# First unit of a gated recurrence: its last head pair's gates and decays through the gaps and a DMA, and the second unit's first steps placed ahead of the first up-projection

## The chip, the cores and the metric

The kernel runs on one core of a Trainium2 chip. The core has TensorE (PE, with its weight loads PEld), VectorE (DVE), ScalarE (ACT), GpSimd (POOL) and SyncE (SP); SP and ACT issue the DMAs here. Times are device microseconds (us) of one execution. The kernel before takes 575.21 us, the median of three runs (574.94 to 575.88).

## The reference

A gated linear recurrence over 768 tokens, for 4 batches of 8 heads of size 48, then a two-layer network with an ELU on 3072 tokens of width 384. The network's two weights are float64, the rest is float32.

```python
f = 1.0 / (1.0 + np.exp(-f_logit))
for t in range(S):
    state = f[:, :, t, :, None] * state + np.einsum('bhd,bhe->bhde', k[:, :, t], v[:, :, t])
    y[:, :, t] = np.einsum('bhd,bhde->bhe', q[:, :, t], state)
x = y.transpose(0, 2, 1, 3).reshape(B * S, H * D)
h = x @ w_in                                    # 384 x 2048
g = np.where(h > 0.0, h, np.exp(np.minimum(h, 0.0)) - 1.0)
out = g @ w_out                                 # 2048 x 384
```

## The kernel before

**Units.** The tokens are cut into 12 units of 256. For each unit the recurrence becomes matmuls over four chunks of 64 tokens. Eight heads lie as four pairs (p = 0 to 3): a pair takes 96 of the 128 partitions, and 32 partitions are gaps. `gates` (L611) turns f's logits into 1/f with two ACT instructions, `grow` (L627) makes their running product with a scan on DVE, `fall` (L632) its reciprocal on DVE. `scale` (L621) multiplies a pair of k by the product and a pair of q by the reciprocal, on POOL. `transposed` (L672) transposes two pairs of k on PE and copies them to kn on ACT. `advance` (L728) makes the four state increments, `step` (L687) adds them up on DVE, `scores` (L704) and `mask` (L721) make the causal products within a chunk, `outputs` (L744) and `carried` (L762) the unit's output, which ACT copies to xt. For unit 0 `first_outputs` (L789) does the last two.

**Where pair 3 lives.** In unit 1 and later, the gates of pair 3 are not loaded as a pair of their own: they are loaded into the gap partitions of pairs 0 to 2, so that three scans and three reciprocals do all heads. `move` (L637) then copies them by two DMAs of 48 rows from the gaps to pair 3's place, once for the products (which = 0) and once for the reciprocals (which = 1). In the kernel before, unit 0 is the exception: all four pairs of f are loaded as they are, with four scans, four reciprocals and no move.

**Weights.** The float64 weights come in 16 items, sorted by when they are needed: item 0 is the first block of w_in, item 1 the second, item 2 the third, item 3 the first block of w_out. `fetch` (L537) loads one into one of seven places of `area`. `split` (L559, two DVE instructions), `lower` (L572, one on ACT) and `merge` (L578) make float32 words of it. merge runs on POOL for items from M0 = 3 on and on DVE for items 0 to 2, and then fetches the item seven further on. `bits`, which split writes and merge reads, has two buffers.

**Order.** The start is written out by hand (L1051 to L1131). `warm` (L1042) issues matmuls of 512 columns on the identity that compute nothing. From then on a loop of steps T runs over pairs of feed-forward blocks: an even T is an `up` (L928), an odd one from 5 on a `down` (L960) two blocks behind; `elu` (L943) is a DVE instruction after the two of ACT in `exped` (L921). What a plan holds for step T (`at_step`) is issued ahead of that step's up or down. A1 gives the steps of unit 1: transposes at its first number (before: at step 1, as a plan entry), then advance, steps, scores and mask, outputs, carried. Splits and lowers of the items from 2 on follow at the ends of steps, their merges in the plan. Engines run their instructions in this order, each waiting for semaphores. The DMAs of SP and ACT share eight semaphores, and a DMA that takes one over waits until the earlier DMA on it has landed.

**The start, in order.** ACT: unit 0's gates in three pieces, kn copies, unit 1's first half of the gates, the first state, lower(0), output copies, lower(1). DVE: memsets, four scans, four reciprocals, split(0), steps, mask, merge(0), the last step, unit 1's three scans, split(1), two reciprocals of unit 1, merge(1). SP: f, k, q of unit 0, f of unit 1, v, item 0, then k, q, v of unit 1, item 1, then item 7 (by merge(0)), the move of unit 1, items 2 to 6. PE: three warms, unit 0's transposes, one warm, advance of pairs 0 and 1, scores of pair 0, and so on with a warm between blocks, first_outputs, a warm, up(0).

Of the kernel before, what the change touches and what calls it, by code (L numbers as in the profile page):

```python
# [356 lines left out]
def fast(ctx: ExitStack, tc: tile.TileContext, q, k, v, f_logit, w_in, w_out, out, flag, outer):  # L357
# [18 lines left out]
    nc = tc.nc  # L376
# [18 lines left out]
    AHEAD = 7  # L395
    WA = 1
    M0 = 3
    Q1 = 4
    W0 = 3
    HOLD = 2  # L400
    A1 = (2, 4, 5, 7, 8, 9)
    D2 = (14, 16, 18, 20)
    A2 = (22, 24, 24, 26, 27, 28)
    D3 = (-7, -5, -3, -1)
# [25 lines left out]
    def load(u, names="fkqv"):  # L430
        b, s0 = u // UPB, (u % UPB) * U
        for n in names.replace("v", ""):
            to = qkf[u % NB][n][MAIN]
            frm = src[n][b, :, :, s0 : s0 + U].rearrange("(p r) d s -> (r d) p s", r=2)
            if n == "f" and u:
                to, frm = to[:, 0:NKT, 0], frm[:, 0:NKT]
            elif n == "f":
                to = to[:, :, 0]
            nc.sync.dma_start(out=to, in_=frm)
            for r in range(2 if n == "f" and u else 0):  # L440
                nc.sync.dma_start(
                    out=qkf[u % NB][n][GAP[r] : GAP[r] + PAD, 0:NKT, 0],
                    in_=src[n][b, 2 * NKT + r, :, s0 : s0 + U].rearrange("(i j) s -> i j s", i=PAD),
                )
        if "v" in names:
            nc.sync.dma_start(
                out=vs[u % NB][:, :, PAD : PAD + DM], in_=v[b, s0 : s0 + U].rearrange("(c t) n -> t c n", t=W)
            )
# [6 lines left out]
    def blank(i, *engines, zeros=None):  # L455
        for j, e in enumerate(engines):
            w = HP // len(engines)
            for n in "kq":
                e.memset(qkf[i][n][:, j * w : (j + 1) * w], 0.0)
        if i:  # L460
            (zeros or engines[-1]).memset(qkf[i]["f"][:, NKT], 1.0)
        else:
            engines[-1].memset(qkf[i]["f"][:, :, 0], 50.0)

    start = ctx.enter_context(ExitStack())
    start.enter_context(tc.manual_schedule())
# [92 lines left out]
    def split(n):  # L559

        if not wide or n >= NFT:
            return
        raw = raws[n]
        hi = raw.bitcast(I32)[:, 1::2]
        bits = held[n] = sb.tile([128, 2 * DM], I32, tag="bits", name=f"bits{n}")
        nc.vector.tensor_scalar(  # L566
            out=bits[:], in0=hi, scalar1=3, scalar2=0x3FFFFFF8,
            op0=ALU.logical_shift_left, op1=ALU.bitwise_and,
        )
        nc.vector.tensor_scalar(out=hi, in0=hi, scalar1=-(2**30), scalar2=None, op0=ALU.bitwise_and)  # L570

    def lower(n):  # L572

        if wide and n < NFT:
            raw = raws[n]
            nc.scalar.activation(raw.bitcast(U16)[:, 2::4], raw.bitcast(U32)[:, 0::2], AF.Copy, scale=2.0**-29)
# [34 lines left out]
    def gates(u, pieces=(NKT,), bias=1):  # L611

        p = 0
        for n in pieces:
            a = qkf[u % NB]["f"][:, p : p + n, 0]
            nc.scalar.activation(a, a, AF.Exp, scale=-1.0)
            if bias:
                nc.scalar.activation(a, a, AF.Copy, bias=1.0)
            p += n

    def scale(u, *todo):  # L621

        t = qkf[u % NB]
        for n, p, e in todo:
            e.tensor_tensor(out=t[n][:, p], in0=t[n][:, p], in1=t["f"][:, p, "kq".index(n)], op=ALU.mult)  # L625
# [6 lines left out]
    def fall(u, p):  # L632

        f = qkf[u % NB]["f"]
        nc.vector.reciprocal(f[:, p, 1], f[:, p, 0])  # L635
# [17 lines left out]
    def watch(u):  # L653
        nc.vector.scalar_tensor_tensor(
            out=fine[:], in0=qkf[u % NB]["f"][:, 0:NKT, 0, U - 1 :], scalar=LIMIT, in1=fine[:],
            op0=ALU.is_le, op1=ALU.mult,
        )

    def watch_last(u):
        nc.vector.scalar_tensor_tensor(  # L660
            out=fine[:, 0:1], in0=qkf[u % NB]["f"][:, NKT:, 0, U - 1 :], scalar=LIMIT, in1=fine[:, 0:1],
            op0=ALU.is_le, op1=ALU.mult,
        )

# [7 lines left out]
    def transposed(u, h, bank, pairs=(0, 1)):  # L672

        if 0 in pairs:
            pts[u, h] = ps.tile([128, 2, NW, 128], FP32, tag=bank, name=f"psT{u}_{h}")
            kns[u, h] = sb.tile([128, 2, NW, 128], FP32, tag="kn", name=f"kn{u}_{h}")
        for p in pairs:
            for w in range(NW):
                nc.tensor.transpose(  # L679
                    pts[u, h][:, p, w], in_=qkf[u % NB]["k"][:, 2 * h + p, w * W : (w + 1) * W], identity=ident[:]  # L680
                )
        p = slice(pairs[0], pairs[-1] + 1)
        nc.scalar.copy(kns[u, h][:, p], pts[u, h][:, p])
# [3 lines left out]
    def step(u, c):  # L687

        if u % UPB == UPB - 1 and c == NC - 1:
            return  # L690
        new = pus[u][c % 2][:, c // 2]
        box = boxes[(u * NC + c) % len(boxes)]
        s = box[:].rearrange("n (p d) -> n p d", d=64)[:, 0:HP, PAD:]
        if u % UPB or c:
            old = sts[u, c][:].rearrange("n (p d) -> n p d", d=64)[:, 0:HP, PAD:]
            nc.vector.tensor_tensor(out=s, in0=new, in1=old, op=ALU.add)
        else:
            nc.scalar.copy(s, new)
        if c == NC - 1:
            end = qkf[u % NB]["f"][:, :, 1, U - 1 :].broadcast_to([128, HP, D])  # L700
            nc.vector.tensor_tensor(out=s, in0=s, in1=end, op=ALU.mult)
        sts[(u, c + 1) if c < NC - 1 else (u + 1, 0)] = box

    def scores(u, banks=("a0", "a1"), pairs=range(HP), pc=None):  # L704

        t = qkf[u % NB]
        if pc is None:
            ats[u] = sb.tile([128, 2, NW, HP, C], FP32, tag="at", name=f"at{u}", bufs=1)
            pc = [ps.tile([128, NW, HP, C], FP32, tag=banks[r], name=f"psS{u}_{r}") for r in range(2)]
        for p in pairs:  # L710
            for w in range(NW):
                for b in range(2):
                    cols = slice(w * W + b * C, w * W + b * C + C)
                    for r in range(2):
                        nc.tensor.matmul(  # L715
                            pc[r][FULL[b], w, p], lhsT=t["k"][FULL[r], p, cols], rhs=t["q"][FULL[r], p, cols],
                            start=True, stop=True,
                        )
        return pc
# [322 lines left out]
    def warm(n, bank="m0"):  # L1042

        pw = ps.tile([128, 4, 128], FP32, tag=bank, name="psW")
        for _ in range(n):
            nc.tensor.matmul(  # L1046
                pw[:], lhsT=ident[:], rhs=ident[:].unsqueeze(1).broadcast_to([128, 4, 128]), start=True, stop=True
            )


    gates(0, (1, 1, 2))  # L1051
    fetch(0)
    load(1, "kqv")
    for n in range(1, HOLD):
        fetch(n)
    warm(W0, "m3")
    for p in range(HP):
        grow(0, p)
        scale(0, ("k", p, nc.gpsimd))
        transposed(0, p // 2, f"m{p // 2}", (p % 2,))  # L1060
    fall(0, 0)
    scale(0, ("q", 0, nc.gpsimd))
    warm(WA, "m3")
# [5 lines left out]
        vs[0][:, :, PAD : PAD + NKT * 2 * D].rearrange("t w (p r d) -> t w p r d", r=2, d=D)[:, :, :, 0],  # L1069
    )  # L1070
    fall(0, 1)
    scale(0, ("q", 1, nc.gpsimd))
    fall(0, 2)
    fall(0, 3)
    advance(0, (2,))
    warm(1)
    scores(0, None, (1,), pc)
    scale(0, ("q", 2, nc.gpsimd))
    advance(0, (3,))
    warm(1)  # L1080
    scores(0, None, (2,), pc)
    nc.gpsimd.tensor_copy(
        padded_v[:, :, :, PAD : 2 * PAD].rearrange("t w (r j) k -> t w r j k", r=2),
        vs[0][:, :, PAD + NKT * 2 * D : PAD + DM].rearrange("t w (r k j) -> t w r j k", r=2, j=NKT),
    )
    scale(0, ("q", NKT, nc.gpsimd))
    warm(1)
    scores(0, None, (NKT,), pc)
    warm(1)
    split(0)  # L1090
    for c in range(NC - 1):
        step(0, c)
    lower(0)
    mask(0, pc)
    merge(0)
    step(0, NC - 1)
    a = qkf[1]["f"][:, 0:NKT, 0]
    nc.vector.tensor_scalar_add(a, a, 1.0)
    for p in range(NKT):
        grow(1, p)  # L1100
    move(1, 0, nc.sync)
    split(1)
    for c in range(NC - 1):
        nc.gpsimd.tensor_copy(
            padded_s[:, c, :, PAD : 2 * PAD],
# [4 lines left out]
        nc.gpsimd.memset(area[:, HOLD:].bitcast(I32)[:, :, 0:1], 0)  # L1110
    for n in range(HOLD, AHEAD):
        fetch(n)
    first_outputs(0)
    first_outputs(1)
    warm(1)
    lower(1)
    fall(1, 0)
    scale(1, ("k", 0, nc.gpsimd), ("k", 1, nc.gpsimd), ("k", 2, nc.gpsimd), ("q", 0, nc.gpsimd))
    fall(1, 1)
    merge(1)  # L1120
    scale(1, ("k", NKT, nc.gpsimd))
    watch(0)
    watch_last(0)
    at_step(1, lambda: transposed(1, 0, "a0"), lambda: transposed(1, 1, "a1"))
    at_step(1, lambda: scale(1, ("q", 1, nc.gpsimd)))
    at_step(1, lambda: fall(1, 2))
    at_step(1, lambda: scale(1, ("q", 2, nc.gpsimd)))
    at_step(1, lambda: move(1, 1, nc.scalar))
    at_step(1, lambda: watch(1))
    at_step(Q1, lambda: scale(1, ("q", NKT, nc.gpsimd)))  # L1130
    attention(1, (), A1)  # L1131
    for n in range(1, NFT):
        t = max(needs[n][0] - 2, 0)
        if n > 1:
            at_step(t, lambda n=n: merge(n))
        if n > 1:
            later.setdefault(max(t - 2, 0), []).append(n)
    at_step(4, lambda: load(2))
# [89 lines left out]
```

## Time and profile before

| | |
|---|---|
| median of 3 runs | 575.21 us |
| the profiled execution | 574.94 us |
| its span in the trace | 573.2 us |
| PE busy | 552.4 us, 96% of the span |
| PEld / DVE / POOL / ACT busy | 502.8 / 394.0 / 292.0 / 229.9 us |
| mean granted clock of TensorE | 0.989 |
| PE's share of the chain of waits | 89% |
| first up-projection matmul (L937) starts | 29.34 us |
| first down-projection matmul (L969) starts | 46.64 us |

The busy time by stage gives for a stretch of the span how long each engine worked; where PE's number is the stretch itself, PE sets the pace. The chain of waits goes back from the last instruction through what released each. The timeline gives start, length, engine, line and operands, and in brackets how long the engine had been idle and who ended it.

### The profile page before, as it was taken

To read this page: it belongs to the slowest core of one execution; us is meant where nothing else is said; L and a number is where in the kernel's file an instruction comes from. 1 tells how busy PE (TensorE), PEld (TensorE's weight loads), DVE (VectorE), ACT (ScalarE), POOL (GpSimd) and SP (SyncE) were. 2 spreads that over 40 slices of the span, in tenths; PEclk is the share of its full clock that TensorE was granted. 3 is DMA by queue.
4 is the path that set the end of the run, shared out by engine and by line. 5 is a ranking of instruction groups with operands and counts; after the bars stand their busy time and mean duration, and the time that the engine had idled before them with its cause. 6 is when DMAs were issued, how large, how long until landed. Compare 5 with 4: busy or idle time off the path is not lost.

```text
span 573.2 us, 15184 instructions
## 1 busy us (share of the span) xinstructions
PE 552.4 (96%) x6220; PEld 502.8 (88%) x6220; DVE 394.0 (69%) x755; ACT 229.9 (40%) x419; POOL 292.0 (51%) x543
## 2 busy tenths in 40 slices
PE   5968899999999999999999999999999999999996
PEld 2546677777999999999999999999999999999996
DVE  6887555564794885786786776776786777655543
ACT  3265855443343343333433433343253243233331
POOL 7335536971357257257257347348348348325332
PEclk9899999999999999999999999999999999999999
DMA  7789970032006216216216206206206303201001
GB/s 193 192 234 281 217 228 16 2 92 74 24 10 152 84 37 153 85 35 153 85 23 166 86 12 176 86 9 179 85 3 172 99 2 77 77 9 35 29 1 35
DMA packets 37614, 53.07 MB, mean 93 GB/s; under 512 B 3584, under 2 KB 27360, under 8 KB 37536
## 3 DMA queue, kind: packets, MB, share of 16 engines
q1 hardware_dynamic: 36992, 51.62, 34.0%
q8 instruction: 51, 0.84, 0.6%
q10 hardware_dynamic: 544, 0.39, 0.3%
q14 instruction: 27, 0.22, 0.1%
HBM read 44.04 MB, written 4.72 MB: 85 GB/s over the span
## 4 chain that ended last, share of the span: by engine, by line
PE 89%; DMA 3%; DVE 3%; POOL 2%; issue 1%; ACT 1%; SPq 0%; ACTq 0%; DVEq 0%; POOLq 0%
PE psH L892 34%; PE psM L991 33%; PE psM L969 6%; PE psH L937 5%; PE psS L715 2%; PE psU_a L738 2%; PE psY L773 2%; PE psY L753 2%; PE psT L679 2%; DMA f<-f 1%; PE psW L1046 1%; DMA area<-in_moe_w_in_dram 1%; POOL wi L585 1%; DMA f<-in_f_logit_dram 1%; DVE bits L566 1%
## 5 line engine op out<-in xcount | busy, mean ns | idle before, releaser
L892 PE MATMUL psH<-xt,wi 128*128 128x128 f32 (+1 forms) x960 | 177.1, 293 | 0.0
L956 POOL TENSOR_TENSOR sums<-gg 128x128 f32<-128x128 f32 x160 | 69.6, 456 | 210.4 <-DVE gg L946 199.3
L892 PEld LDWEIGHTS psH<-xt,wi 128*128 128x128 f32 x960 | 135.9, 192 | 0.8
L924 ACT ACTIVATE gg<-hh 128x512 f32<-128x512 f32 x80 | 50.5, 631 | 205.4 <-DVE hh L914 137.9
L892 PE MATMUL psH<-xt,area 128*128 128x128 f32 x640 | 110.5, 275 | 0.0
L892 PEld LDWEIGHTS psH<-xt,area 128*128 128x128 f32 x640 | 96.9, 192 | 4.1
L901 DVE TENSOR_TENSOR hh<-psH,u 128x256 f32<-128x256 f32 x80 | 33.8, 422 | 88.8 <-ACT u L899 88.8
L991 PE MATMUL psM<-area,sums 128*128 128x192 f32 x480 | 91.1, 326 | 0.0
L991 PEld LDWEIGHTS psM<-area,sums 128*128 128x128 f32 x480 | 80.2, 190 | 0.0
L991 PE MATMUL psM<-wo,gg 128*128 128x192 f32 x320 | 68.1, 335 | 0.0
L635 DVE RECIPROCAL f<-f 128x256 f32<-128x256 f32 x37 | 64.2, 1745 | 1.0
L925 ACT ACTIVATE gg<-gg 128x512 f32<-128x512 f32 x96 | 60.6, 631 | 3.0
L946 DVE SCALAR_TENSOR_TENSOR gg<-gg,hh 128x512 f32<-128x512 f32 x80 | 55.7, 696 | 1.5 <-ACT gg L925 1.5
L991 PEld LDWEIGHTS psM<-wo,gg 128*128 128x128 f32 x320 | 50.2, 190 | 1.9
L914 DVE TENSOR_TENSOR hh<-psH,u43h 128x256 f32<-128x256 f32 (+1 forms) x160 | 49.6, 352 | 2.7
L937 PE MATMUL psH<-xt,wi 128*128 128x256 f32 x192 | 46.5, 394 | 1.9 <-DVE wi L585 1.1
L625 POOL TENSOR_TENSOR k<-k,f 128x256 f32<-128x256 f32 x48 | 40.0, 836 | 13.7 <-DVE f L630 13.0
L937 PEld LDWEIGHTS psH<-xt,wi 128*128 128x128 f32 x192 | 37.0, 196 | 10.4 <-ACT xt L830 1.3
L956 POOL TENSOR_TENSOR sums<-gg,sums 128x128 f32<-128x128 f32 x80 | 42.7, 534 | 6.3
L899 ACT COPY u<-psH 128x128 f32<-128x128 f32 x80 | 21.1, 264 | 59.4 <-PE psH L892 59.4
L969 PE MATMUL psM<-wo,gg 128*128 128x384 f32 x128 | 44.2, 488 | 0.0
L914 DVE TENSOR_TENSOR u43h<-psH,hh 128x256 f32<-128x256 f32 x80 | 33.8, 422 | 13.5 <-PE psH L892 13.1
(100 smaller groups left out, 746.5 us busy)
## 6 DMA issues: line engine op xcount, KB each, us to landing
area<-in_moe_w_out_dram SPq DMA_DIRECT2D x8, 768.0 KB, 6.5
again<-in_moe_w_in_dram SPq DMA_DIRECT2D x16, 384.0 KB, 4.3
again<-in_moe_w_out_dram SPq DMA_DIRECT2D x16, 384.0 KB, 3.5
k<-in_k_dram SPq DMA_DIRECT2D x12, 384.0 KB, 4.9
q<-in_q_dram SPq DMA_DIRECT2D x12, 384.0 KB, 5.9
v<-in_v_dram SPq DMA_DIRECT2D x12, 384.0 KB, 6.3
area<-in_moe_w_in_dram SPq DMA_DIRECT2D x8, 576.0 KB, 8.8
out_dram<-o SPq DMA_DIRECT2D x38, 96.0 KB, 1.7
```

Of the source, the lines that this page charges most:

```text
L625: e.tensor_tensor(out=t[n][:, p], in0=t[n][:, p], in1=t["f"][:, p, "kq".index(n)], op=ALU.mult)
L635: nc.vector.reciprocal(f[:, p, 1], f[:, p, 0])
L892: nc.tensor.matmul(to, lhsT=lhs, rhs=rhs, start=(n == 0), stop=True, skip_group_check=True)
L901: add = lambda to, x, y: nc.vector.tensor_tensor(out=to, in0=x, in1=y, op=ALU.add)
L914: add = lambda to, x, y: nc.vector.tensor_tensor(out=to, in0=x, in1=y, op=ALU.add)
L924: nc.scalar.activation(g[:], h, AF.Relu, scale=-1.0)
L925: nc.scalar.activation(g[:], g[:], AF.Exp, scale=-1.0)
L937: nc.tensor.matmul(ph[:, i], lhsT=wi[j][:, kt, i * 128 : (i + 1) * 128], rhs=xts[m][:, kt, :], start=(kt == 0), stop=(kt == NKT - 1),)
L946: nc.vector.scalar_tensor_tensor(out=g[:], in0=g[:], scalar=-1.0, in1=phs.pop(P), op0=ALU.add, op1=ALU.max)
L956: nc.gpsimd.tensor_tensor(out=s[:, i], in0=x, in1=y, op=op)
L969: nc.tensor.matmul(pm[t][:], lhsT=g[:, i, t * 128 : (t + 1) * 128], rhs=wo[:, 2 * j + i, :], start=(j == 0 and i == 0), stop=(j == NP - 1 ...
L991: nc.tensor.matmul(pm[bank][:, half * DH : (half + 1) * DH], lhsT=x, rhs=y, start=first, stop=(j == NP - 1), skip_group_check=True,)
```

## The change

All edits concern the first 60 us or so.

- Unit 0's f is loaded and blanked as that of the other units: pairs 0 to 2 and two small loads into the gaps, a memset of pair 3's place alone. Its gates are two pieces (pair 0, pairs 1 and 2) instead of three; it has three scans and three reciprocals, and two moves on ACT's queue (which = 0 after the first kn copies, which = 1 after the third reciprocal). `watch_last`, which looked at pair 3's last product, goes, as the gaps are watched with the others.
- k's pair 3 is scaled after the move, and its transpose stands after four warms. There are twelve warms in place of nine in the start.
- Unit 1's scans, its SP move and its first reciprocal come before unit 0's steps and mask; split(0), lower(0) and merge(0) come after the mask.
- The loop that fetches items 2 to 6 comes before merge(0), which fetches item 7.
- Unit 1's k scaling, transposes, third reciprocal and second move, which were partly plan entries of step 1, stand in the start ahead of up(0). Its q of pair 3 is scaled at step 1 instead of 4. merge(1) becomes a plan entry of step 0. A1 is (2, 3, 4, 6, 7, 9) instead of (2, 4, 5, 7, 8, 9).

M0, the item from which GpSimd merges, is 3 in both kernels.

```diff
-    A1 = (2, 4, 5, 7, 8, 9)
+    A1 = (2, 3, 4, 6, 7, 9)
...
-            if n == "f" and u:
+            if n == "f":
                 to, frm = to[:, 0:NKT, 0], frm[:, 0:NKT]
-            elif n == "f":
-                to = to[:, :, 0]
             nc.sync.dma_start(out=to, in_=frm)
-            for r in range(2 if n == "f" and u else 0):
+            for r in range(2 if n == "f" else 0):
...
-        if i:
-            (zeros or engines[-1]).memset(qkf[i]["f"][:, NKT], 1.0)
-        else:
-            engines[-1].memset(qkf[i]["f"][:, :, 0], 50.0)
+        (zeros or engines[-1]).memset(qkf[i]["f"][:, NKT], 1.0)
...
-    gates(0, (1, 1, 2))
+    gates(0, (1, 2))
...
-    for p in range(HP):
+    for p in range(NKT):
         grow(0, p)
         scale(0, ("k", p, nc.gpsimd))
-        transposed(0, p // 2, f"m{p // 2}", (p % 2,))
+        if p < 2:
+            transposed(0, 0, "m0", (p,))
+    move(0, 0, nc.scalar)
+    transposed(0, 1, "m1", (0,))
     fall(0, 0)
...
-    scale(0, ("q", 1, nc.gpsimd))
+    scale(0, ("k", NKT, nc.gpsimd), ("q", 1, nc.gpsimd))
     fall(0, 2)
-    fall(0, 3)
+    move(0, 1, nc.scalar)
+    warm(4)
+    transposed(0, 1, "m1", (1,))
     advance(0, (2,))
-    warm(1)
     scores(0, None, (1,), pc)
     scale(0, ("q", 2, nc.gpsimd))
     advance(0, (3,))
-    warm(1)
     scores(0, None, (2,), pc)
...
-    scale(0, ("q", NKT, nc.gpsimd))
-    warm(1)
-    scores(0, None, (NKT,), pc)
-    warm(1)
-    split(0)
-    for c in range(NC - 1):
-        step(0, c)
-    lower(0)
-    mask(0, pc)
-    merge(0)
-    step(0, NC - 1)
     a = qkf[1]["f"][:, 0:NKT, 0]
     nc.vector.tensor_scalar_add(a, a, 1.0)
     for p in range(NKT):
         grow(1, p)
     move(1, 0, nc.sync)
-    split(1)
+    scale(0, ("q", NKT, nc.gpsimd))
+    warm(2)
+    scores(0, None, (NKT,), pc)
+    warm(1)
+    fall(1, 0)
+    for c in range(NC - 1):
+        step(0, c)
+    mask(0, pc)
+    step(0, NC - 1)
+    split(0)
...
     for n in range(HOLD, AHEAD):
         fetch(n)
+    fall(1, 1)
     first_outputs(0)
+    lower(0)
+    merge(0)
     first_outputs(1)
+    scale(1, ("k", 0, nc.gpsimd), ("q", 0, nc.gpsimd), ("k", 1, nc.gpsimd), ("k", 2, nc.gpsimd))
+    scale(1, ("k", NKT, nc.gpsimd))
+    split(1)
+    transposed(1, 0, "a0")
     warm(1)
+    transposed(1, 1, "a1")
     lower(1)
-    fall(1, 0)
-    scale(1, ("k", 0, nc.gpsimd), ("k", 1, nc.gpsimd), ("k", 2, nc.gpsimd), ("q", 0, nc.gpsimd))
-    fall(1, 1)
-    merge(1)
-    scale(1, ("k", NKT, nc.gpsimd))
     watch(0)
-    watch_last(0)
-    at_step(1, lambda: transposed(1, 0, "a0"), lambda: transposed(1, 1, "a1"))
-    at_step(1, lambda: scale(1, ("q", 1, nc.gpsimd)))
-    at_step(1, lambda: fall(1, 2))
-    at_step(1, lambda: scale(1, ("q", 2, nc.gpsimd)))
-    at_step(1, lambda: move(1, 1, nc.scalar))
-    at_step(1, lambda: watch(1))
-    at_step(Q1, lambda: scale(1, ("q", NKT, nc.gpsimd)))
+    scale(1, ("q", 1, nc.gpsimd))
+    fall(1, 2)
+    scale(1, ("q", 2, nc.gpsimd))
+    move(1, 1, nc.scalar)
+    watch(1)
+    at_step(1, lambda: scale(1, ("q", NKT, nc.gpsimd)))
     attention(1, (), A1)
     for n in range(1, NFT):
         t = max(needs[n][0] - 2, 0)
-        if n > 1:
-            at_step(t, lambda n=n: merge(n))
+        at_step(t, lambda n=n: merge(n))
```

More of the change, by code (lines that the diff above doesn't have):

```diff
@@ L397, in fast @@
     M0 = 3
-    Q1 = 4
     W0 = 3
     HOLD = 2
-    A1 = (2, 4, 5, 7, 8, 9)
+    A1 = (2, 3, 4, 6, 7, 9)
     D2 = (14, 16, 18, 20)
@@ L655, in watch @@
             out=fine[:], in0=qkf[u % NB]["f"][:, 0:NKT, 0, U - 1 :], scalar=LIMIT, in1=fine[:],
[L656 to L661, printed above, removed]
             op0=ALU.is_le, op1=ALU.mult,
```

## The prediction

> **What bounds the kernel now.** I read the busy time by stage first. The columns are the stretch, its length, then busy us and instruction count of PE, PEld, DVE, ACT and POOL, then the granted clock.
>
> ```profile
> core 0: us, PE busy (x) PEld busy (x) DVE busy (x) ACT busy (x) POOL busy (x), PEclk, DMA share, GB/s
> 8.40:11.80 3.40, 1.20 (x5) 0.40 (x4) 2.91 (x4) 1.78 (x4) 2.77 (x3) 0.97 1.12 278
> 11.80:18.20 6.40, 5.73 (x71) 3.40 (x72) 6.40 (x5) 1.49 (x3) 3.97 (x8) 0.50 1.10 242
> 29.34:42.30 12.96, 8.27 (x97) 6.56 (x97) 11.50 (x15) 7.42 (x7) 4.30 (x5) 1.00 0.93 236
> 42.30:45.60 3.30, 3.30 (x8) 2.67 (x9) 3.11 (x3) 1.91 (x4) 1.92 (x1) 0.50 1.07 291
> 45.60:65.30 19.70, 16.41 (x237) 11.70 (x236) 14.20 (x21) 14.26 (x14) 11.33 (x7) 1.00 1.00 271
> 65.30:75.00 9.70, 9.70 (x41) 7.06 (x38) 3.46 (x5) 7.85 (x10) 3.64 (x3) 1.00 0.67 131
> ```
>
> From 65.3 us on PE does not idle again before the tail of the last output. Before that it has holes, and its clock is halved twice, after a stretch with few matmuls each time. So the change is worth the time by which it moves the start of the full stretch. I read the chain of waits next (start, length, what), for the early holes.
>
> ```profile
> 1.79 0.90 POOL f L463
> 2.69 0.02 issue
> 2.71 3.87 DMA f<-in_f_logit_dram
> ...
> 31.12 5.20 DMA area<-in_moe_w_in_dram
> ...
> 40.05 6.88 DMA f<-f
> ...
> 47.74 1.86 POOL wi L585
> 49.61 0.02 issue
> 49.63 2.19 DVE bits L566
> ```
>
> Three transfers carry it: the first gates, which wait for a memset; the third weight item; and unit 1's moved decays. The timeline shows why the third item is late, and whom it stops.
>
> ```profile
> 24.79 0.39 SPq L547 DMA_DIRECT2D area<-in_moe_w_out_dram  x1
> ...
> 28.48 1.30 SPq L642 DMA_DIRECT2D f<-f  x2
> ...
> 29.87 0.53 SPq L549 DMA_DIRECT2D area<-in_moe_w_in_dram  x1
> ...
> 39.34 1.16 ACT L683 COPY kn<-psT 128x512 f32<-128x512 f32 x2
> ...
> 40.07 0.31 PE L738 MATMUL psU_a<-v,kn 64*64 64x48 f32 x2 [2.67 <-ACT kn L683]
> ```
>
> merge(0) stands ahead of the fetch loop, so item 7 (24.79) is fetched before item 2 (29.87), and SP's move of unit 1 waits in between for DVE's scans. Item 2's last piece lands at 36.32. ACT stands in lower(2) until its split, and the kn copies behind it hold PE's advance(1).
>
> PE's blocks start at (timeline): up0 29.34, up1 34.57, advance 40.07, up2 42.26, down0 46.64, up3 49.65, scores 53.62, down1 55.15, outputs 59.21, up4 60.89, carried 64.03, down2 65.30, done 68.15. Full-clock costs from the chain: up 2.59, down 2.58, an attention block 1.09, transposes 0.87. Five ups, three downs, four blocks and the transposes are 25.9; the stretch is 38.8, so 12.9 us are lost in it: 1.8 before up1, 2.9 before advance, 1.1 before up2, 1.8 by the halved clock in up2, 0.4 before up3, 1.4 + 0.4 around scores, 1.5 + 0.6 around outputs, about 1 in the rest.
>
> **The change, in order of time.**
>
> *Words merged by GpSimd.* M0 is 3 in both files and each item keeps its engine: nothing.
>
> *Opening.* Pair 3's gates go into the gaps, and the memset touches pair 3's place alone, which no load writes; in the changed order the f load waits for nothing. SP can issue it when the other queues begin, at about 0.9 instead of 2.71. It is now three DMAs; issues by the rows of unit 1's load are 0.48 + 0.70 + 0.58. With the 3.87 to landing it is there at 4.8 to 4.9 instead of 6.58: 1.7 early. k follows 1.5 later, as before (8.08 - 6.58), at 6.4. ACT then has 0.42 + 0.42 + 0.61 + 0.63, DVE three scans of 0.69 instead of four. But PE's three warm matmuls (1.68 each at the start) hold it to 8.3, so transposes 0 to 2, one warm, advance(0, 1) and the first scores end at about 12.3; before, 17.0.
>
> *Four warms, and pair 3 by DMA.* Four warms of 1.05 fill PE to 16.5 (19.4 at half clock). Behind them in PE's queue stands pair 3's transpose, for k3, which waits for ACT's new move of the scanned gates, issued about 10.5 and 11.3. The trace has two prices for such a move: 2.2 from issue to landing on SP's queue at 28.5, with nothing ahead of it, and 6.9 on ACT's queue at 39.3, with SP's loads ahead; the xt moves at 66.6 took 6.1 and 5.5. That is 13 to 18; k3's scaling (0.73 to 1.0) behind it ends at 14 to 19, near the end of the warms either way. The second move waits for the third reciprocal (three of 1.7 from 8.9, so 14.2), is issued at 14.25 and 15.0, and lands between 17.2 and 21.9. I take 21.4, the loaded row, since SP's loads have kept the DMA engines busy without a break from 4 to 24 us. POOL's q3 (0.73) then ends at 22.2, the last scores at 22.5, and mask starts at 22.75: before 22.61. So the 1.7 won in the opening and the fourth scan and reciprocal are eaten by this move. With the short price, mask follows the warms at 20.6.
>
> The Trainium skill, "DMA: Bandwidth & Descriptors", section on queues, rings and completion order, says that each DMA engine takes turns between the queues it has work for, packet by packet. By that rule a small move on ACT's queue would not stand behind SP's backlog, and the time would be that of the short price, 566. The row of 6.9 at 39.3 speaks against it here.
>
> SP's unit 1 move and fetches stand behind these moves too, since they reuse their semaphores: to about 21.9. The padding memset of the area (POOL, after the states) frees the fetches at 22.9 anyway.
>
> *From mask to up0.* Before, 6.73. Now split(0) and lower(0) come after mask: mask 1.3, two state steps 0.72, split 1.0 + 0.6 under POOL's scaling, lower 1.93, then the three xt copies (0.48 + 0.96) behind it on ACT; with the gaps 7.5. merge(0) (0.95) runs beside xt. PE meanwhile does unit 1's transposes and a warm (0.87 + 1.05), covered by that wait. up0 at 30.3: 1.0 late.
>
> *From up0 on.* The loop now fetches items 2 to 6 before merge(0) fetches 7. Item 2 needs 6.45 from issue to the last landing (29.87 to 36.32), so 22.9 gives 29.4: 7 early, before anybody asks. The transposes and kn copies lie ahead of lower(1), so the 2.9 before advance go, with the 0.87 itself and the 1.8 of clock that followed the hole. unit 1's last move is issued at 31.5 and lands at 34 to 38.4, ahead of POOL's first merge at 39.7; before, q3 at 47.06 held merge 4 (47.74). What stays, by the same rows in the new order:
> - up1: xt to 30.2, kn 1.2, lower(1) 1.93, merge(1) 0.95, so 34.55, against 32.9: 1.7.
> - up2: split(2) to 35.7, lower to 37.7; DVE is in split(3) and elu to 38.2, merge(2) to 39.2, against 38.2: 1.1.
> - scores: DVE's splits 4 and 5 (one at 2.1 beside POOL's merge), elu, steps of 0.36, against down0's end at 44.5: 0.9 + 0.4.
> - outputs: splits 6 and 7, elu and mask to 52.4, against up3's end at 49.4: 2.3 + 0.7.
>
> That is 7.1 of loss, on 25.05 of work: about 32.0 instead of 38.8. With the 1.0 of up0, down2 ends at 62.3 instead of 68.15. The attention steps moved in A1 keep the order that this list uses; watch_last (0.16) goes. After that PE is full and nothing differs, except that every later load and merge is issued as much earlier; the xt move (6.1 in the loaded row) must land before up6, four blocks later, which had 0.3 to spare before.
>
> **Sum.** -5.8, of which I keep -5.5 for the 0.3 that the walk rounds. The profiled execution is 574.94 (span 573.2 and 1.74 around it), the median of the runs 575.21. 574.94 - 5.5 = **569.4**.
>
> **Rivals.**
> - *The moves are short* and the clock stays full: mask at 20.6, up0 at 28.0, the later waits a little shorter (5.9): -9, **566**. For it: the 2.2 row. Against: 6.9, 6.1 and 5.5 under load.
> - *The clock halves* at 11.8 to 18.2 again: the warms end at 19.4, mask at 23.8, up0 at 31.0: 0.7 more, **570.1**. For it: it did, after 1.20 busy us in 3.4. Against: in the new order PE is busy about 2.3 of these 3.4, and 16.41 of 19.70 kept it full.
> - *The weight chain is the bound*: DVE's splits waited 5.1 us for POOL's merges (two bits buffers), ACT 12.2 for splits. If that cadence sets the full stretch, only T's 0.87 goes and up0's 1.0 comes: **575**, up to 577 if the splits also stretch beside POOL in the start. Against: the chain names two DMAs of 5.20 and 6.88 where these chains stood still.
> - *Slower:* pair 3's second move waits for the whole of SP's queue and more. Each us of landing beyond the assumed one shifts mask, up0 and all after it. From a landing at 27 (12.4 after issue) the gain is gone; at 28.5 it is **576.5**. Against: the longest row is 6.9, and SP, held by the same semaphores, can add nothing meanwhile, so the queue drains by about 22.
>
> **How the numbers follow.** Forecast 0.40; short moves 0.14; halved clock 0.20; weight chain 0.14 (0.06 within 0.2%, 0.08 above); late move 0.12. Faster by over 0.2% (1.15 us, about what a measurement here can tell from none): 0.74; within: 0.06; slower: 0.20. The range runs from the short moves, 565.8, to the upper part of the weight chain, 576.0, and leaves out the late move and a little at either end.
>
> **What would show it.** f's first load issued before 1.5 us; ACT's moves at 10 to 15 landing 6 us later or 2; mask near 22.7 and up0 near 30.3; no wait for kn before advance(1), and item 2 landed before 30; the end of down2 near 62.3 with no halved clock at 40 to 46. It is wrong if up0 starts after 33, or if the holes after up0 still sum to over 11.

## The result and the profile after

| | before | after |
|---|---|---|
| median | 575.55 us (4 runs, 574.94 to 575.99) | 569.69 us (4 runs, 568.47 to 570.13) |
| ratio, 95% interval | | 0.9896 (0.9876 to 0.9916) |
| profiled execution | 574.94 us | 569.28 us |
| its span | 573.2 us | 567.3 us |
| mean granted clock | 0.989 | 0.995 |
| mask starts | 22.61 | 21.15 |
| up0 starts | 29.34 | 29.66 |
| third down (down2) ends and the next up starts | 68.0 | 62.1 |
| from there to the end of the span | 505.2 | 505.2 |

The rows from the span down are of the one profiled execution each. The change is 1.04% faster, 5.9 us. All of it lies ahead of the end of down2: what follows is equal to 0.1 us.

The busy time by stage of the kernel after, with the columns of the prediction's first view (length, busy us and count of PE, PEld, DVE, ACT, POOL, then clock, DMA share, GB/s). The DMA share is the mean busy share of the core's 16 DMA engines; its readings come out as high as 1.1, so about 1 means full:

```profile
8.40:11.80 3.40, 2.35 (x9) 0.87 (x8) 3.40 (x3) 0.74 (x2) 2.24 (x4) 1.00 1.11 268
11.80:18.20 6.40, 5.87 (x106) 3.30 (x106) 5.33 (x6) 1.49 (x3) 2.51 (x5) 1.00 1.11 224
29.66:46.00 16.34, 12.64 (x112) 9.15 (x111) 13.34 (x21) 12.73 (x12) 5.75 (x5) 1.00 0.87 219
46.00:62.06 16.06, 16.00 (x230) 12.15 (x231) 12.50 (x15) 11.79 (x15) 9.28 (x5) 0.89 1.03 289
```

Neither of the two halvings of before is there: the clock stays full at 11.8 to 18.2 and in the early ups. A new one falls at 46. From 46.0 on PE is full (16.00 of 16.06), which it was from 65.3 on before.

The chain of waits of the kernel after (start, length, what):

```profile
2.01 2.60 DMA f<-in_f_logit_dram
...
10.98 4.99 DMA f<-f
...
19.91 8.10 DMA area<-in_moe_w_in_dram
...
28.03 5.40 DMA area<-in_moe_w_in_dram
...
38.88 2.19 POOL wo L579
```

Of the three transfers that carried the chain before, the gates' load lands 2.0 earlier (at 4.61 instead of 6.58), the third weight item is fetched 10 earlier (first issue at 19.91 instead of 29.87), and the 6.88 for unit 1's moved decays is gone. New in it are the 4.99 of unit 0's own move and a piece of item 4 (28.03).

The timeline of SP, then that of PE, show the order of the fetches and what is left of the waits (start, length, instruction, and in brackets the idle time before and who ended it):

```profile
19.91 0.32 SPq L543 DMA_DIRECT2D area<-in_moe_w_in_dram  x1
...
28.64 0.59 SPq L541 DMA_DIRECT2D area<-in_moe_w_out_dram  x1
37.88 0.32 SPq L543 DMA_DIRECT2D area<-in_moe_w_in_dram  x1
...
39.55 0.53 SPq L541 DMA_DIRECT2D area<-in_moe_w_out_dram  x1
```

```profile
25.13 0.66 PE L806 MATMUL psY<-at,padded_v 64*32 64x64 f32 x33 [1.41 <-issue]
...
33.67 2.83 PE L925 MATMUL psH<-xt,wi 128*128 128x256 f32 x12 [1.25 <-DVE wi L579]
36.43 1.15 PE L726 MATMUL psU_a<-v,kn 64*64 64x48 f32 x64
37.79 2.83 PE L925 MATMUL psH<-xt,wi 128*128 128x256 f32 x12 [0.21 <-DVE wi L579]
41.12 1.24 PE L957 MATMUL psM<-wo,gg 128*128 128x384 f32 x3 [0.49 <-POOL wo L579]
```

Item 2 (19.91) is fetched 10 us earlier than before, and items 3 to 6 follow it (28.64 is item 5, 37.88 item 6). Item 7, which was first before, comes last, at 39.55. The advance at 36.43, which waited 2.67 for ACT's kn copies before, waits for nothing. What remains in these lines are waits for merges, 1.25, 0.21 and 0.49.

What the early fetches filled is seen in the busy time by stage of the same two stretches, of before and then of after. Read the DMA share, the number before the last:

```profile
22.00:34.00 12.00, 10.19 (x209) 7.14 (x208) 11.29 (x14) 4.84 (x8) 4.82 (x6) 1.00 0.51 137
34.00:44.00 10.00, 6.02 (x80) 4.88 (x81) 8.39 (x13) 5.81 (x6) 3.20 (x3) 0.92 1.04 280
```

```profile
22.00:34.00 12.00, 8.74 (x193) 6.85 (x193) 9.09 (x14) 7.17 (x11) 2.77 (x4) 1.00 1.02 234
34.00:44.00 10.00, 9.25 (x96) 6.52 (x94) 7.69 (x10) 7.30 (x7) 4.81 (x3) 1.00 0.73 207
```

Before, the DMA engines stood idle for half of 22 to 34 us, and PE stood for weights in 34 to 44. After, they work through the first stretch, and PE's busy time in the second goes from 6.02 to 9.25.

### The profile page after: what moved, and what is told of

Read it like the earlier page. It is cut to its first block, busy times and chain, and to the rows that moved or that the text cites. A ratio compares the mean times of both kernels' runs of the same rounds, so it can differ in the third digit from the quotient of the medians.

```text
span 567.3 us, 15209 instructions
## 1 busy us (share of the span) xinstructions
PE 551.5 (97%) x6226; PEld 502.4 (89%) x6226; DVE 389.3 (69%) x752; ACT 228.9 (40%) x417; POOL 289.7 (51%) x543
## 4 chain that ended last, share of the span: by engine, by line
PE 91%; DMA 4%; POOL 1%; DVE 1%; issue 1%; ACT 1%; SPq 0%; ACTq 0%; DVEq 0%; POOLq 0%
PE psH L880 35%; PE psM L979 33%; PE psM L957 7%; PE psH L925 6%; DMA area<-in_moe_w_in_dram 2%; PE psS L703 2%; PE psY L741 2%; PE psY L761 2%; PE psU_a L726 2%; PE psT L667 2%; DMA f<-f 1%; POOL k L619 1%; DMA f<-in_f_logit_dram 0%; POOL wo L579 0%; POOL q L619 0%
## 5 line engine op out<-in xcount | busy, mean ns | idle before, releaser
L629 DVE RECIPROCAL f<-f 128x256 f32<-128x256 f32 x36 | 62.8, 1748 | 1.0
L619 POOL TENSOR_TENSOR k<-k,f 128x256 f32<-128x256 f32 x48 | 38.7, 808 | 13.7 <-DMA f<-f 7.0
```

## The experiments

Two theories. **A** (the prediction): the gain comes after up(0), from the fetch order and from unit 1's steps placed ahead; unit 0's part breaks even. **B**: the gain comes from unit 0's part, which loads its gates earlier and frees DVE of a scan and a reciprocal. Gains are medians against the kernel before, run beside them on the same chip (575.73 for e1 to e4, 575.18 for e5 to e8, 575.64 for e9 to e12). The ratio is an estimate of its own and can differ from the quotient of the medians (e5: 0.9907, and 570.34 / 575.18 = 0.9916). The intervals of the ratios are some 0.0015 to 0.002 to either side, so a difference of under 1 us between two of these kernels is none that they can tell.

| run | median, us | gain, us | ratio, 95% interval | mask | up0 | down2 ends |
|---|---|---|---|---|---|---|
| the change | 569.69 | 5.9 | 0.9896 (0.9876 to 0.9916) | 21.15 | 29.66 | 62.1 |
| e1 | 571.07 | 4.7 | 0.9917 (0.9900 to 0.9934) | 23.03 | 30.99 | 64.3 |
| e2 | 574.40 | 1.3 | 0.9983 (0.9969 to 0.9997) | 21.13 | 28.76 | 67.0 |
| e3 | 572.30 | 3.4 | 0.9951 (0.9932 to 0.9969) | 20.55 | 28.67 | 63.1 |
| e4 | 571.25 | 4.5 | 0.9926 (0.9909 to 0.9943) | 22.77 | 30.89 | 63.2 |
| e5 | 570.34 | 4.8 | 0.9907 (0.9888 to 0.9926) | 23.90 | 33.76 | 66.4 |
| e6 | 574.22 | 1.0 | 0.9982 (0.9966 to 0.9997) | 20.50 | 31.21 | 66.9 |
| e7 | 570.01 | 5.2 | 0.9907 (0.9887 to 0.9927) | 20.89 | 30.27 | 61.3 |
| e8 | 570.84 | 4.3 | 0.9924 (0.9908 to 0.9940) | 19.33 | 27.94 | 62.2 |
| e9 | 572.70 | 2.9 | 0.9945 (0.9930 to 0.9960) | 22.34 | 29.05 | 63.5 |
| e10 | 569.52 | 6.1 | 0.9891 (0.9871 to 0.9912) | 21.21 | 31.12 | 63.2 |
| e11 | 569.60 | 6.0 | 0.9891 (0.9878 to 0.9905) | 19.91 | 28.74 | 62.8 |
| e12 | 570.89 | 4.8 | 0.9904 (0.9888 to 0.9920) | 19.53 | 26.40 | 66.2 |

The last three columns are of the one profiled execution. That of e5 took 573.75, of e9 574.60, of e11 571.75 and of e12 573.31: each is the slowest of its runs, so its stages are not those of its median. From the end of down2 to the end of the span most of these executions take 505.2 to 505.7, but e3, e7 and e8 take 506.2 to 506.4 and e11 507.3, as PE waits once more, ahead of up6, for xt's move (0.5 to 1.5), and e9 takes 509.4, with a wait of 2.08 for a weight and the clock halved behind it. So their last column shows more than their gain.

**e1: all but unit 0's part.** The changed kernel with unit 0's four pairs loaded, scanned and inverted as before.

```diff
-    gates(0, (1, 2))
+    gates(0, (1, 1, 2))
...
-    for p in range(NKT):
+    for p in range(HP):
         grow(0, p)
...
-    move(0, 0, nc.scalar)
...
-    move(0, 1, nc.scalar)
-    warm(4)
+    fall(0, 3)
```

> The changed kernel with unit 0's part as before: pair 3's gates loaded as they are, four scans, four reciprocals, no moves, its warms. All else as changed. Theory A (the prediction's): the gain is won after up0, by unit 1's steps and the fetch order, and unit 0's moves only break even, so this stays within 1 us of the changed kernel, 569 to 571. Theory B: the gain comes from unit 0, whose earlier load and three reciprocals leave DVE free at 12.9 instead of 17.8 us, and only that lets unit 1's scans and reciprocal (4.3 us) run ahead of mask. Then mask starts at 23 or later instead of 21.15 and the time is 571.7 or more.

It keeps 4.7 of the 5.9, and lies between the two theories' ranges (A up to 571, B from 571.7). So most of the gain is not unit 0's.

**e2: unit 0's part alone**, in the kernel before.

```diff
-    gates(0, (1, 1, 2))
+    gates(0, (1, 2))
...
-    for p in range(HP):
+    for p in range(NKT):
         grow(0, p)
...
-    fall(0, 3)
+    move(0, 1, nc.scalar)
+    warm(4)
```

> The kernel before with unit 0's part alone as changed (gaps, moves, three reciprocals, its warms); unit 1's steps, the fetch order and the plan as before. Theory A: no gain, 574.5 to 576. Theory B: most of the gain, 572 or less. If both parts are needed, mask comes at about 21.2 instead of 22.6 and up0 at 28, and the time is 573.5 to 574.5.

1.3, and 1.3 + 4.7 is the 5.9 of the whole within 0.2, closer than these runs can tell: the two parts add up. Theory A has the larger part; but unit 0's part doesn't break even, it wins 1.3 (the interval leaves out 1), and this much of B holds.

**e3: unit 1's steps back in the plan.** The changed kernel with unit 1's transposes, last reciprocal and second move at step 1, its q of pair 3 at step 4, and the old A1.

```diff
-    transposed(1, 0, "a0")
     warm(1)
-    transposed(1, 1, "a1")
...
+    at_step(1, lambda: transposed(1, 0, "a0"), lambda: transposed(1, 1, "a1"))
...
-    A1 = (2, 3, 4, 6, 7, 9)
+    A1 = (2, 4, 5, 7, 8, 9)
```

> The changed kernel with unit 1's transposes, last reciprocal and second move back in the plan of step 1, its q of pair 3 at step 4 and the old A1. Theory A: the wait for kn before advance(1) and the 0.87 us of transposes come back, 572.5 to 574.5. Theory B: under 1 us of loss, 569.5 to 570.7.

Gain 3.4 instead of 5.9, so these places are worth some 2.4 in the changed kernel. The advance, though, waits 0.33 for kn there, not 2.67: with item 2 early, lower(2) no longer holds up ACT, and the kn copies behind it are nearly in time. What comes back are the transposes (0.87) between up0 and up1 and a wait of 1.32 for GpSimd's merge.

**e4: the opening as late as before.** One memset more, which f's first load waits for.

```diff
         (zeros or engines[-1]).memset(qkf[i]["f"][:, NKT], 1.0)
+        if i == 0:
+            engines[-1].memset(qkf[i]["f"][:, 0:NKT, 0], 1.0)
```

> The changed kernel with one memset more, of what unit 0's load of f writes, so that this load waits until about 2.9 us as before. Theory A (and the prediction's step, that the moves eat what the opening wins): up0 moves by under 0.5 us, 569.5 to 570.3. Theory B: all of unit 0 and the loads behind it come 2.1 us later, and so does up0: 571.5 to 572.

f's load is issued at 2.96 instead of 0.80; mask comes 1.6 later, up0 1.2, down2 1.1, and 1.4 of the gain is gone by the gains, 1.6 by the medians, nearer to B's range than to A's. The intervals of e4 and of the changed kernel overlap, so the size is rough: the opening is worth about what unit 0's part is worth.

**e5: lower(0) ahead of the first outputs**, and merge(0) with it, item 7 still fetched last. **e6: the same with item 7 first**: it differs from e5 in the fetch order alone.

```diff
-        fetch(n + AHEAD)
+        if n:
+            fetch(n + AHEAD)
...
+    lower(0)
+    merge(0)
-    for n in range(HOLD, AHEAD):
+    for n in range(HOLD, AHEAD + 1):
         fetch(n)
...
     first_outputs(0)
-    lower(0)
-    merge(0)
```

e6 has the move of lower(0) and merge(0) alone: the loop ends at AHEAD, and merge(0), now ahead of it, fetches item 7.

> The changed kernel with lower(0) and merge(0) ahead of the fetch loop and of the first outputs; items 2 to 7 are fetched in that order still. If lower(0) behind the first output copies is what holds up(0) (26.17 in the changed kernel's trace, with its operand ready before), up(0) starts 0.3 to 1 earlier and the time is 568.7 to 569.4. If PE's stall at the first padded_v matmuls or the xt copies hold it, nothing changes: 569.7.

> As the run before it, with one difference: item 7 is fetched ahead of items 2 to 6, by merge(0), as in the kernel before. Theory A (the fetch order is a main part of the gain, as the prediction has it): item 2 lands 2 to 5 later than 28.6 and up1 to up2 stand for it, 1 to 3 slower than the run with item 7 last: 570.5 to 572.5. Rival (the gain is that unit 1's transposes and copies lie ahead of lower(1), and the order of the fetches is idle): the same time as with item 7 last, within 0.4.

e5 cannot be told from the changed kernel: in its profiled execution, with lower(0) ahead, PE's `q,state` matmuls wait 2.14 for `between`, which now stands behind lower(0) on ACT. e6 loses 3.9 against e5 (the intervals lie apart), more than the 1 to 3 expected. From up0 to the end of down2 its profile takes 35.7, that of e5 32.6 and that of the changed kernel 32.4. SP's timeline in e6:

```profile
18.45 1.30 SPq L636 DMA_DIRECT2D f<-f  x2
27.02 0.40 SPq L541 DMA_DIRECT2D area<-in_moe_w_out_dram  x1
```

Item 7 goes into the place that merge(0) frees. Ahead of items 2 to 6, whose places are free, it holds SP from 19.8 to 27.0, and the DMA share of 22 to 34 is 0.52, as in the kernel before. What this costs shows late. In PE's timeline of e6, and in its chain of waits:

```profile
50.47 1.78 PE L703 MATMUL psS<-q,k 64*64 64x64 f32 x42 [4.70 <-issue]
```

```profile
31.87 7.36 DMA f<-f
39.25 6.64 DMA area<-in_moe_w_out_dram
```

The transfer at 39.25 is item 5, which was fetched at 28.64 in the changed kernel. With item 7 ahead of it, its fetch is the one that takes over the semaphore of unit 1's second move and waits for that move to land (39.23); its split, an elu and the state steps stand behind it on DVE, and the scores behind those. How the 3.9 divides between the late start and this second wait is not shown. The place of that one line is the largest single piece.

**e7: fewer warms**, four left out; they compute nothing.

```diff
-    warm(2)
     scores(0, None, (NKT,), pc)
-    warm(1)
...
     transposed(1, 0, "a0")
-    warm(1)
     transposed(1, 1, "a1")
```

> The changed kernel without the three warm matmuls around unit 0's last scores and the one between unit 1's transposes. If warms on PE hold the mask rather than the move of the reciprocals (which landed at 18.3, not at 21.4 as the prediction took it), the last scores come about 1 earlier, mask at 20.0, up(0) at 28.7 or later, and the time is 568.7. If the move or POOL's scaling behind it holds the mask, it stays: 569.7. If the clock halves in the first ups, for less work in front of them, 571 or more.

Not to be told from the changed kernel. GpSimd's and PE's stretch there:

```profile
19.53 0.72 POOL L619 TENSOR_TENSOR q<-q,f 128x256 f32<-128x256 f32 x1 [1.00 <-DMA f<-f]
```

```profile
18.20:22.00 3.80, 1.25 (x36) 0.84 (x36) 1.82 (x4) 0.32 (x1) 2.80 (x8) 1.00 1.09 262
22.00:29.00 7.00, 6.29 (x166) 5.37 (x167) 5.64 (x8) 2.50 (x4) 3.17 (x5) 0.54 1.00 251
```

Without warms PE is busy 1.25 of 3.8 us and its clock is halved in the next stretch. Yet the mask stands at 20.89: the q scaling waits for the second move (landed 19.40, against 18.26 in the changed kernel). In the changed kernel q was scaled by 19.28 and the last scores started behind the warms at 20.57, so there the warms did hold the mask by some 1.2; the later landing takes that place in this execution, and in the time no cost of the warms can be told.

**e8: unit 0's moves on SP's queue**, ahead of item 0 and of unit 1's k, q, v and item 1.

```diff
-    fetch(0)
-    load(1, "kqv")
-    for n in range(1, HOLD):
-        fetch(n)
...
-    move(0, 0, nc.scalar)
+    move(0, 0, nc.sync)
+    fetch(0)
...
-    move(0, 1, nc.scalar)
+    move(0, 1, nc.sync)
+    load(1, "kqv")
+    for n in range(1, HOLD):
+        fetch(n)
```

> The changed kernel with unit 0's two moves on SP's queue, the first ahead of item 0, the second ahead of unit 1's k, q, v and item 1, instead of on ACT's queue. If a move lands when what SP issued before it has landed, they land near 12 to 13 and 16 to 17 instead of 16.0 and 18.3, and unit 1's k, q, v and item 1 come 2 to 3 later. Prediction's step (the second move sets mask): mask 1 to 2 earlier, 568.0 to 569.0. Rival (PE's warms set it by now): mask stays near 21.1 and the later item 1 costs nothing or up to 1: 569.7 to 570.7.

The moves land at 11.6 and 16.5, instead of 16.0 and 18.3 in the changed kernel. Mask is 1.8 earlier, up0 1.7, and nothing is won: the wait moves on to GpSimd and to PE behind it.

```profile
38.53 0.73 POOL L619 TENSOR_TENSOR q<-q,f 128x256 f32<-128x256 f32 x1 [7.43 <-DMA f<-f]
39.23 1.83 POOL L579 TENSOR_TENSOR wo<-bits,area 128x768 int32<-128x768 int32 x1
```

```profile
41.11 2.85 PE L957 MATMUL psM<-wo,gg 128*128 128x384 f32 x8 [2.12 <-POOL wo L579]
```

The q scaling of unit 1's pair 3 waits for unit 1's second move. It was issued 1.5 earlier and landed 0.3 later (38.40) than in the changed kernel: the last load that SP had issued before it landed at 37.83 here and 37.67 there. The merge for down0 stands behind it on GpSimd, its words ready since 36.8, and down0 starts where it did.

**e9: the early fetches alone**, in the kernel before: unit 1's scans, its SP move and the fetch loop ahead of split(0).

```diff
+    a = qkf[1]["f"][:, 0:NKT, 0]
+    nc.vector.tensor_scalar_add(a, a, 1.0)
+    for p in range(NKT):
+        grow(1, p)
+    move(1, 0, nc.sync)
+    if wide:
+        nc.gpsimd.memset(area[:, HOLD:].bitcast(I32)[:, :, 0:1], 0)
+    for n in range(HOLD, AHEAD):
+        fetch(n)
     split(0)
...
     merge(0)
     step(0, NC - 1)
-    a = qkf[1]["f"][:, 0:NKT, 0]
-    nc.vector.tensor_scalar_add(a, a, 1.0)
-    for p in range(NKT):
-        grow(1, p)
-    move(1, 0, nc.sync)
...
-    if wide:
-        nc.gpsimd.memset(area[:, HOLD:].bitcast(I32)[:, :, 0:1], 0)
-    for n in range(HOLD, AHEAD):
-        fetch(n)
     first_outputs(0)
```

> The kernel before with one part of the change: unit 1's scans, its move and the loop that fetches items 2 to 6 stand ahead of split(0), so SP takes item 2 before item 7. Unit 1's transposes stay at step 1, behind lower(1), and unit 0's part stays. The order of the fetches was worth 3.9 when it was undone in the changed kernel, the places of unit 1's steps 2.6, and both together 4.7, so they overlap. If the fetches alone free the later waits: 2 to 3 faster than before, 572.2 to 573.2. If the copies of unit 1's transposes, still behind lower(2) on ACT, hold PE all the same: 574.5 to 575.5.

2.9, in the middle of what was expected: half of the whole change. Its PE, in the timeline:

```profile
35.83 0.31 PE L738 MATMUL psU_a<-v,kn 64*64 64x48 f32 x2 [0.46 <-ACT kn L683]
```

The DMA share of 22 to 34 is 0.94, and the advance's wait for kn falls from 2.67 to 0.46 although the copies still stand behind lower(2). The kernels fall into two groups by that one share: 0.51 (before), 0.65 (e2) and 0.52 (e6) with gains of 0 to 1.3, and 0.82 to 1.05 in all others, with gains of 2.9 to 6.1.

**e10: q of pair 3 at step 4** in the changed kernel, and **e11: that and e8's moves.**

```diff
-    at_step(1, lambda: scale(1, ("q", NKT, nc.gpsimd)))
+    at_step(4, lambda: scale(1, ("q", NKT, nc.gpsimd)))
```

> The changed kernel with unit 1's q of pair 3 scaled at step 4 instead of step 1, so that GpSimd's first merge (item 3) no longer stands behind the landing of unit 1's second move. In the changed kernel's trace the merge began 0.47 after its words were there, so down0 comes at most 0.5 earlier: 569.2, or 569.7 if the next split gives it back.

> Both: unit 0's moves on SP's queue (which by itself brought mask 1.8 and up(0) 1.7 earlier, but down0 at the same 41.1 and the same time) and q of pair 3 at step 4. If GpSimd's merge behind the landing of unit 1's second move ate the 1.7 (38.5 for the q scaling, with item 3's words lowered at 36.8), down0 comes at 38.8 to 39.5 and the time is 568.5, 2.0 to 2.3 under the run with the moves on SP alone. If the splits and merges behind it set the pace anyway (two buffers of bits), 570 to 571.

e10 is the changed kernel's time; the wait of 0.49 ahead of down0 is gone in its profile, as expected, but up0 came later in that execution (31.12, with the clock halved just before it). In e11 down0 comes at 39.62 and up3 at 44.31, 1.5 and 3.6 earlier than in the changed kernel, so the merge was what ate e8's lead in the profiles. Its median is 1.2 under e8's and the ratio goes from 0.9924 to 0.9891, but that is again the changed kernel's time. The chain of waits of e11's profiled execution, 2.2 above its median, shows what stands next:

```profile
29.74 7.41 DMA area<-in_moe_w_in_dram
...
41.87 5.87 DMA area<-in_moe_w_out_dram
...
52.00 4.46 PE psM L957 x8
...
62.10 7.23 DMA xt<-xt
```

DVE now waits for the weights' landing itself. PE then stands 3.07 before the outputs, runs down1 at the halved clock (4.46 instead of 2.58) and waits 1.50 for xt's move before up6.

**e12: e11 with unit 1's second transposes behind up(0).**

```diff
     warm(1)
-    transposed(1, 1, "a1")
...
             up(P)
+            if not T:
+                transposed(1, 1, "a1")
```

> As the run before it, and unit 1's second pair of transposes behind up(0) instead of ahead of it. With the moves on SP, up(0)'s operands were there at 26.0 and it waited to 27.9 for the transpose of pair 3, whose k waits for unit 1's first move (landed 26.75). If up(0)'s start decides, 0.6 to 1.5 faster than the run before: 567.2 to 568. If the merges decide, the same as the run before.

up0 starts at 26.40, 3.3 earlier than in the changed kernel, and the time is 570.89: no gain, by the median 1.3 more than e11, which the intervals do not separate. In these runs an earlier up0 buys nothing more.

## Why the prediction was right, and where not

It said 569.4, and 569.69 came, by the likeliest of its cases. Its sum was right in part by luck, because two errors offset each other: up0 came 0.6 earlier than it said, and the stretch from up0 to the end of down2 was 32.6 instead of 32.0. (The prediction counts to the end of down2's last matmul, 68.15 before and 62.23 after; the tables here to the start of the next block. Its own terms give 32.15 for that stretch, 34.28 instead of 34.55 for up1's start, and 31.3 instead of 31.0 for up0 at halved clock; none of these changes the account.) By its steps:

- **Opening.** Right: f's load issued at 0.80, landed at 4.61 (4.8 to 4.9 expected), no halved clock at 11.8 to 18.2 (PE busy 2.35 of the 3.4 before, 2.3 expected).
- **"So the 1.7 won in the opening and the fourth scan and reciprocal are eaten by this move."** This step failed in its size, by two terms. The reciprocals ended at 12.94, not 14.2, since f came earlier still and DVE began them at 7.99; and the second move took 4.7 from the issue of its last DMA (13.57 to 18.26), not the 6.4 it was given (15.0 to 21.4). So mask was at 21.15 instead of 22.75, and unit 0's part wins 1.3 (e2) instead of nothing. The choice between the two prices was right in kind, but the price is no fixed row: these moves landed 0.3 to 0.6 behind the last load that SP had issued before them (for the second one unit 1's k, which landed at 17.65). The short price was no different: the move at 28.48 did not have "nothing ahead of it", as item 7, issued at 24.79, landed at 29.83, 0.9 before it.
- **From mask to up0.** 8.5 instead of 7.5. Not counted was PE's stall of 1.41 ahead of the `padded_v` matmuls (the first line of PE above), which holds `between`, lower(0) and the xt copies behind it. Putting lower(0) first brings another wait (e5).
- **Fetch order.** Right, and the largest term: item 2 landed at 28.6 (29.4 expected; 36.3 before), and the order alone is worth 3.9 in the changed kernel (e6 against e5) and, with the scans it needs, 2.9 in the one before (e9).
- **"The transposes and kn copies lie ahead of lower(1), so the 2.9 before advance go."** The wait went, but by e9 most of it goes with the fetches alone, without moving the copies. The prediction saw two causes in one wait: lower(2) stood on ACT *because* item 2 was late. The places are still worth some 2.4 (e3).
- **Losses after up0.** 7.5 in sum, 7.1 expected, but not where they were put: ahead of up1 1.4 (1.7), of up2 0.3 (1.1), of down0 0.7 (none expected), of the scores 1.9 (0.9), from the scores to the end of the outputs 2.6 (3.4), and 0.6 in the rest (none). The 2.6 shows as a halved clock after 46, in the scores, up3 and the outputs, which the prediction did not have; but it mostly fills time in which PE would have stood for DVE. e7 has its clock full there, and its PE stands for DVE's mask, as the prediction said:

```profile
50.50 0.32 PE L741 MATMUL psY<-at,v 64*64 64x64 f32 x2 [1.89 <-DVE at L711]
```

  From its scores (44.23) to the end of its outputs (52.18) e7 takes 7.95, the changed kernel 7.33 (45.59 to 52.92).
- **"lands at 34 to 38.4, ahead of POOL's first merge at 39.7."** It landed at 38.06 as said, but the merge's words were there at 38.41, and the q scaling that waits for it ended at 38.9. PE's wait ahead of down0 is 0.49 in the changed kernel and 2.12 once up0 is earlier (e8). And the move has a second price, which the prediction charged to unit 0's moves but not here. In the waits of SP's queue of the changed kernel:

```profile
SPq L543 <- DMA f<-f: 8.6, 1, 8.6
```

  SP's next fetch, of item 6, takes over that move's semaphore and stands 8.6 us, until 37.88. Its busy time by stage shows the hole that follows:

```profile
36.00:38.00 2.00, 1.78 (x68) 1.36 (x67) 1.55 (x3) 2.00 (x2) 0.00 (x0) 1.00 0.18 52
```

  The DMA engines, at a share of 1.04 in the four us before, fall to 0.18. e11 then stands for weights fetched after this hole. That a move which doesn't hold SP would close it, and what that would bring, was not tried.

The rivals. *Short moves*: e8 gave them, with up0 at 27.9 as that rival said (28.0), and 570.8 instead of 566, since PE then waits 2.12 instead of 0.49 ahead of down0. *Halved clock*: e1 shows it (0.53 at 11.8 to 18.2 after 1.48 busy us in 3.4), the changed kernel not. *Weight chain*: its splits and merges do not set the pace from 46.0 on in the changed kernel (PE busy 16.00 of 16.06), though they are in the waits before; in e11 its transfers carry the chain as well. *Late move*: the chain of waits of e5's profiled execution shows it once:

```profile
14.43 7.98 DMA f<-f
```

The move took 7.98 there, mask came at 23.90, and that execution is 3.4 above its median. So the price was real; in the changed kernel's profiled execution the landing was on the good side of it.

Left open: what e3's 2.4 is made of beyond the 0.87 and the 1.32 that its profile shows, and whether the hole at 36 to 40 can be closed.

## What to carry to other kernels

Ahead of every fetch on an in-order queue, ask what frees the place it writes to: one fetch that waits for a merge, ahead of five that wait for nothing, left the DMA engines half idle for 12 us and cost 3 to 4. Price a small DMA not by its size but by when the last load issued before it, on any queue, lands (2 to 9 us from issue here), and look for who inherits its semaphore. And test a start in both directions: here 1.2 of delay at up0 went with 1.4 of time (e4, with intervals that overlap), and 0.9 to 3.3 of lead won nothing (e8, e11, e12), since a merge, and then the landing of weights, took it up.

## What the runs showed of the hardware

**A small move lands with the backlog of the other queue.** A move is two DMAs of 48 KB each. In the changed kernel ACT's landed at 15.69, 15.98, 17.93, 18.26, 37.87 and 38.06, and the last load that SP had issued before each at 15.09, 15.39, 17.65, 17.65, 37.67 and 37.67: 0.2 to 0.6 behind it. The same holds on SP's own queue (e8: 16.32 and 16.49 behind item 0's 16.15), and for most moves of the other kernels. In six of the fourteen executions one or both parts of unit 1's second move came 0.4 to 3.4 ahead of that load (before, e2, e6, e9, e11, e12), and some moves came up to 3.1 behind it (e5). The issue counts for little: 1.5 earlier in e8 (31.12 instead of 32.58), and 0.3 later in landing. The Trainium skill ("DMA: Bandwidth & Descriptors", section on queues, rings and completion order) lets the DMA engines take turns between queues packet by packet, by which ACT's moves would pass SP's backlog; these runs show it in few cases.

**The clock after one short gap.** In the changed kernel PE idles 1.63 us ahead of the scores at 45.59, is busy 1.66 of the 3.4 us to 46.0, and then runs at about half clock. Its busy time by stage:

```profile
42.60:46.00 3.40, 1.66 (x7) 0.67 (x6) 3.19 (x7) 2.19 (x2) 0.96 (x2) 1.00 1.04 320
46.00:49.40 3.40, 3.37 (x66) 3.01 (x67) 3.36 (x4) 1.22 (x3) 1.64 (x1) 0.52 1.05 272
```

In the stretch of 8.4 to 11.8, 1.20 (before) and 1.48 (e1) busy us of 3.4 were followed by half clock as well, 1.93 (e4) and 2.35 (the changed kernel) were not. The Trainium skill, "TensorE: Matmul & The Clock Gate", section "Why this matters for your kernels", asks for no idle gap over about 3 us; here 1.63 sufficed. How busy PE was tells more than the longest gap: in the kernel before, no gap from 8.4 to 11.6 was over 0.83, and the clock was halved after it; in e8 PE stood 2.12 from 38.99 to 41.11, and its clock stayed full until 46.1. Where a stretch begins matters too. In each trace the changes of the clock lie whole multiples of 3.41 us apart (in the changed kernel at 8.60, 46.14 and 49.56). Counted in such steps up to 76 us, over all fourteen traces, the step ahead of each halving had PE busy for 0 to 1.8 us, and the steps at full clock that no halving followed for 1.6 or more: the border is near half.

**A stall that waits for nothing in the trace.** PE stood 1.41 (after), 0.70 (e2), 1.19 (e3), 1.02 (e4), 1.27 (e6), 1.19 (e10) and 0.17 us (e7) within the `padded_v` matmuls, marked "issue"; the others have none. Busy DMA engines do not decide it: over the stall their share was 1.06 in the changed kernel but 0.04 in e6, and e8, e11 and e12 have none at 1.06 to 1.08. The traces have a DMA queue of their own for instructions, though. In the changed kernel, from 20 to 26 us:

```profile
q8 instruction: 1, 0.02, 1.5%
```

This one transfer of 16 KB ran from 22.20 to 23.66, and PE went on at 25.13, 1.5 behind its end; in the six other stalls PE went on 1.2 to 1.5 behind the end of such a transfer. In e5, e8, e11 and e12 it ended 3.6 to 4.6 ahead of the first `padded_v` matmul, in before, e1 and e9 1.2 to 1.5 ahead of it. So PE most likely waits for these instructions, but no run moved that transfer by itself, and the cause is not shown.
